# Keys of batches 2 to 4: projected in float16 with tokens on partitions, and turned by the DMA

## The chip, the core and the metric

One core of one Trainium2 chip runs the whole kernel. The metric is device microseconds of that core. The engines are TensorE (PE, with PEld for its weight loads), VectorE (DVE), ScalarE (ACT), GpSimd (POOL) and SyncE (SP), whose queue issues every DMA of this kernel.

## The reference

```python
kv_pool = kv.reshape(B, H // 4, 4, W // 4, 4, C).mean(axis=(2, 4))   # 384x32 -> 96x8 = 768 tokens
k = v = kv_pool.reshape(B, -1, C) @ w_sr                              # 768 x 128 per batch
a = softmax(q @ k.T / sqrt(C))                                        # q: 12288 x 128 per batch
x = (a @ v)                                                           # 4 x 12288 x 128
out = gelu_erf(x @ w_in) @ w_out                                      # 128 -> 2048 -> 128
```

There are 4 batches. The keys (which are the values too) are 768 rows of 128 per batch, made from 12288 pixels by a mean over 4x4 and one 128x128 projection. Everything is float32; the kernel writes its large products as three float16 products of high and low halves.

## The kernel before

A tile is 512 query rows, so a batch has 24 tiles and the kernel 96, numbered `i` = 0 to 95. A tile's work is spread over 16 slots, `f` = 0 to 15, one slot for each 128-wide block of the hidden layer. `slots(i)` yields the work in the order in which each engine gets it. In a slot PE computes one hidden block of tile `i` (`mlp_in`, L765 to L767, three matmuls of 512 columns) and one output block of six slots ago (`mlp_out`, L828 to L830). Scores of tile `i+2` stand in slots 3, 6 and 9, and the first score of tile `i+3` in slot 13 (`score`, L681, six matmuls of 384 columns); the attention product of tile `i+1` stands in slots 10 to 12 (`av`, L741). Every engine works through its own queue in that order, and an instruction that waits holds up what is queued behind it.

A tile's query rows have their own chain: `q_load` (slot 1, L451), the largest value by DVE (`q_max`, slot 5, L479), three passes on POOL that make halves (`q_split`, L502 to L504), a transpose by DMA (`q_turn`, slot 9, L527), and the first score in slot 13 of the same tile `i`. SP also carries the four transposes of the attention weights of a tile (`attn_turn`, L729: two in slot 12, one in slot 15, one in slot 4 of the next tile), the transposes of the output (`o_turn`, L464), the output's stores (L860) and the loads of the next batch's pixels (`kv_load`, L247).

Keys of batch 1 of 4 are made in the kernel's start by a list written out by hand (`START`, tiles 0 to 2). The keys of batches 2 to 4 are made beside the tiles of the batch before, by a table of (tile, slot) that `at` fills (L984 to L1005). With `i0` the second tile of the batch before, for each of six parts `h` of 128 tokens: `kv_load` at tile `i0+2h` slot 1, `kv_sum` on POOL at `i0+2h+1` slot 1, `kv_turn` at `i0+2h+2` slot 2 and `kv_key` at the same tile, slot 11. `kv_turn` (L356) is a float32 transpose on PE, which ACT copies with the factor 1/16 (L358). `kv_key` (L365) is a float32 matmul with `w_sr` as weights, which DVE copies into `kT` (L366), so that channels stand on partitions and tokens along the row. Then `kv_max` (L373) takes the largest value of each channel, and `kv_bound` spreads the largest of all to all partitions: a diagonal matrix on DVE (L380), a float32 matmul by ones (`across`, L386), a reduction on DVE (L391). `kv_high` and `kv_low` (L420, L425) make float16 halves with channels on partitions, as the scores take them, and `kv_val` (L432) is one transpose by DMA of 12 blocks, which makes the halves with tokens on partitions, as `av` takes them.

The PSUM buffer `ps_t` is single, and `kv_turn`, `kv_key` and `across` share it.

Of the kernel before, what the change touches and what calls it, by code (L numbers as in the profile page):

```python
# [16 lines left out]
ALU = mybir.AluOpType  # L17
AX = mybir.AxisListType
# [126 lines left out]
def pooled_attention_mlp(  # L145
# [24 lines left out]
    T = 512  # L170
# [3 lines left out]
    HALVES = (H // P) * 2  # L174
# [20 lines left out]
    kv_h = kv.rearrange("b (h i a) (j w) c -> b h a i j (w c)", i=P // WK, a=R, j=WK)  # L195

    const = ctx.enter_context(tc.tile_pool(name="const", bufs=1))
    stage = ctx.enter_context(tc.tile_pool(name="stage", bufs=6))
# [13 lines left out]
    op = ctx.enter_context(tc.tile_pool(name="op", bufs=1))  # L212
# [28 lines left out]
    st = {}  # L241
# [95 lines left out]
    def kv_sum_part(b, h, i, eng):  # L337
        t = st["kv", b, h][i]
        u = prep.tile([P, 4 * C], F32, tag=f"u{i}", name=f"u_{b}_{h}_{i}")
        eng.tensor_tensor(u, t[:, : 4 * C], t[:, 4 * C :], op=ALU.add)  # L340
        eng.tensor_tensor(u[:, : 2 * C], u[:, : 2 * C], u[:, 2 * C :], op=ALU.add)
        eng.tensor_tensor(u[:, :C], u[:, :C], u[:, C : 2 * C], op=ALU.add)
        st["u", b, h, i] = u[:, :C]
        if i == 1:
            y = prep.tile([P, C], F32, tag=f"y{h % 2}", name=f"y_{b}_{h}")
            eng.tensor_tensor(y, st.pop(("u", b, h, 0)), st.pop(("u", b, h, 1)), op=ALU.add)
            st["y", b, h] = y

    def kv_sum(b, h, eng):

        for i in range(2):
            kv_sum_part(b, h, i, eng)

    def kv_turn(b, h, pool=ps_t, tag="ps_t"):
        ps = pool.tile([P, T], F32, tag=tag, name=f"pp_{b}_{h}")
        nc.tensor.transpose(ps[:, :P], st.pop(("y", b, h)), ident)  # L356
        pT = prep.tile([P, P], F32, tag=f"pT{h % 2}", name=f"pT_{b}_{h}")
        nc.scalar.mul(pT, ps[:, :P], 1.0 / (R * R))  # L358
        st["pT", b, h] = pT

    def kv_key(b, h, pool=ps_t, tag="ps_t", mul=nc.vector.tensor_scalar_mul):
        if h == 0:
            st["kT", b] = prep.tile([P, KEYS], F32, tag="kT", name=f"kT_{b}")
        ps = pool.tile([P, T], F32, tag=tag, name=f"pk_{b}_{h}")
# [619 lines left out]
    def at(i, f, *op):  # L984
        extra.setdefault((i, f), []).append(op)

    for b in range(1, B):
        i0 = TPB * (b - 1) + 1
        for h in range(HALVES):
            i = i0 + 2 * h  # L990
            at(i, 1, "kv_load", b, h)
            at(i + 1, 1, "kv_sum", b, h)
            at(i + 2, 2, "kv_turn", b, h)
            at(i + 2, 11, "kv_last", b, h)
        i1 = i0 + 2 * HALVES + 2
        at(i1, 11, "kv_top", b)
        at(i1, 11, "kv_bound", b, 0)
        at(i1 + 1, 2, "kv_bound", b, 1)
        at(i1 + 1, 11, "kv_bound", b, 2)
        at(i1 + 1, 11, "kv_bound", b, 3)  # L1000
        at(i1 + 1, 12, "mlp_scale", b)
        at(i1 + 1, 12, "out_scale", b)
        at(i1 + 2, 11, "kv_hi", b)
        at(i1 + 2, 12, "kv_lo", b)
        at(i1 + 3, 11, "kv_val", b)  # L1005

    def slots(i):

# [69 lines left out]
    with tc.manual_schedule():  # L1078
        engines = {"dve": nc.vector, "pool": nc.gpsimd}
        copies = {"act": nc.scalar.copy, "dve": nc.vector.tensor_copy}  # L1080
        muls = {"act": nc.scalar.mul, "dve": nc.vector.tensor_scalar_mul,
                "pool": nc.gpsimd.tensor_scalar_mul}
        by = {
            "q_load": q_load, "w_sr": lambda: nc.sync.dma_start(w_sr_sb, w_sr),
            "kv_in": kv_in, "kv_add": lambda h, n=0, m=1, e="dve": kv_add(h, n, m, engines[e]), "kv_pool": kv_pool,
            "kv_pool_out": lambda h, e: kv_pool_out(h, copies[e]),
            "kv_flip": kv_flip, "kv_flip_out": lambda h, e: kv_flip_out(h, copies[e]),
            "kv_nat": kv_nat, "kv_nat_out": lambda n, e: kv_nat_out(n, copies[e]),
            "kv_key": kv_key_first, "kv_key_out": lambda h, e: kv_key_out(h, copies[e]),
            "w_load": w_load, "w_single": w_single, "w_max": w_max, "w_sum": w_sum,  # L1090
            "w_scale": lambda i, step, e="dve": w_scale(i, step, engines[e]),
            "w_hi": lambda j, e: w_hi(j, muls[e]), "w_lo": w_lo,
            "q_turn_first": q_turn_first, "q_out_first": lambda e: q_out_first(copies[e]),
            "score_part": score_part, "evac_part": evac_part, "exp_part": exp_part,
            "turn_part": turn_part,
            "turn_out_part": lambda c, n, e: turn_out_part(c, n, copies[e]),
            "av_part": av_part,
            "parts": lambda step, e="dve": parts(step, engines[e]),
            "join_first": lambda c, e: join_first(c, muls[e]), "join_second": join_second,
            "x_turn": x_turn, "x_first": lambda n, e: x_first(n, copies[e]),  # L1100
            "q_max": q_max, "q_scale": lambda t, e="dve": q_scale(t, engines[e]),
            "q_turn": q_turn, "q_sigma": lambda t, e="dve": q_sigma(t, engines[e]),
            "q_split": q_split, "q_hi": lambda t, e: q_hi(t, muls[e]), "q_lo": q_lo,
            "kv_max": lambda n: kv_max(0, n, 2),
            "kv_high": lambda n, e: kv_high(0, n, 2, muls[e]),
            "kv_bound": lambda b, step, e="dve": (
                kv_bound(b, step) if b else kv_bound(b, step, 2, ps_h, "ps_h", engines[e])),
            "kv_val": kv_val, "mlp_scale": lambda b, e="dve": mlp_scale(b, engines[e]),
            "out_scale": lambda b, e="dve": out_scale(b, engines[e]), "warm": warm,
            "kv_load": kv_load, "kv_sum": lambda b, h: kv_sum(b, h, nc.gpsimd),  # L1110
            "kv_turn": kv_turn, "kv_last": kv_key, "kv_top": kv_max, "kv_hi": kv_high,
            "kv_lo": kv_low, "exp": exp,
            "recips": lambda t, c, n, e="dve": recips(t, c, n, engines[e]),
            "attn_hi": lambda t, c, e="dve": attn_hi(t, c, muls[e]),
            "attn_lo": attn_lo, "attn_turn": attn_turn,
            "x_hi": lambda t, e="dve": x_hi(t, muls[e]), "x_lo": x_lo,
            "score": score, "evac": evac, "mlp_in": mlp_in, "gelu": gelu,
            "gelu_hi": lambda t, p, e="act": gelu_hi(t, p, muls[e]), "rest": rest, "mlp_out": mlp_out, "av": av,
            "o_out": lambda t, e="act": o_out(t, muls[e]), "o_planes": o_planes, "o_turn": o_turn, "o_join": o_join,
            "o_last": o_last,  # L1120
        }
# [37 lines left out]
```

## Time and profile before

| | |
|---|---|
| three timed runs | 2785.69, 2785.78, 2786.09 us |
| median | 2785.78 us |
| span of the profiled execution | 2784.1 us |
| busy: PE, ACT, DVE, POOL | 100%, 90%, 84%, 31% of the span |
| TensorE's granted clock | full speed in all 40 slices |
| DMA engines, mean busy share | 43% of 16 engines |

The profile has the span of its execution, from the first to the last instruction, and no time around it; the median of the timed runs is 1.68 us above that span. "Busy" of PE counts a matmul from its issue to its modelled end, and matmuls overlap, so the cost of a matmul to the queue is the distance between the starts of neighbours and not its duration.

### The profile page before, as it was taken

What the parts mean: (1) busy time and instruction counts of PE and PEld (TensorE: products, weight loads), DVE (VectorE), ACT (ScalarE), POOL (GpSimd) and SP (SyncE); (2) the same over time, 40 slices, a digit from 0 to 9 for tenths busy, and PEclk for the clock granted to TensorE, in tenths of its full rate; (3) what the DMA queues carried; (4) which work ended last, traced back from release to release, by engine and by line L of the source; (5) the groups of instructions that cost most, each with busy time, mean ns of one, the idle gap of its engine ahead of it and who ended that gap; (6) DMA issues with size and microseconds to landing.
All of it is one profiled execution on the core that took longest, in us unless ns stands there. A gap on an engine that the chain in (4) does not pass through costs nothing.

```text
span 2784.1 us, 38177 instructions
## 1 busy us (share of the span) xinstructions
PE 2777.5 (100%) x13720; PEld 1338.0 (48%) x13720; DVE 2349.7 (84%) x3449; ACT 2514.5 (90%) x3419; POOL 867.0 (31%) x826
## 2 busy tenths in 40 slices
PE   9999999999999999999999999999999999999999
PEld 6444444444444444444444444444444444444445
DVE  7888888888888888898888888889888888888786
ACT  7899999999989999998999999899999999899997
POOL 3344442323244343323224343422222232222221
PEclk9999999999999999999999999999999999999999
DMA  7444444344454445344444444433444434343342
GB/s 226 108 105 106 107 108 97 84 106 90 96 117 113 108 104 111 90 91 98 98 106 108 107 106 113 101 95 91 99 95 89 97 89 95 88 99 91 93 89 54
DMA packets 844910, 283.08 MB, mean 102 GB/s; under 512 B 807216, under 2 KB 809776, under 8 KB 843952
## 3 DMA queue, kind: packets, MB, share of 16 engines
q1 hardware_dynamic: 844720, 280.65, 43.2%
q8 instruction: 107, 1.75, 0.3%
q14 instruction: 83, 0.68, 0.1%
HBM read 54.59 MB, written 25.17 MB: 29 GB/s over the span
## 4 chain that ended last, share of the span: by engine, by line
PE 98%; DMA 1%; DVE 0%; POOL 0%; issue 0%; ACT 0%; SPq 0%; POOLq 0%
PE s L681 13%; PE px L741 13%; PE h L765 12%; PE h L766 12%; PE h L767 12%; PE po L830 12%; PE po L829 12%; PE po L828 11%; PE po L819 0%; PE h L762 0%; PE po L806 0%; DMA row<-in_kv_dram 0%; PE s L568 0%; DMA q_v<-q_u 0%; PE warm L325 0%
## 5 line engine op out<-in xcount | busy, mean ns | idle before, releaser
L780 ACT ACTIVATE g<-h,hs 128x512 f32<-128x512 f32 x1520 | 995.2, 681 | 214.6 <-PE h L767 177.1
L788 DVE SCALAR_TENSOR_TENSOR gl<-g,gs,gh 128x1024 f16<-128x1024 f32 x760 | 1003.3, 1333 | 16.1 <-ACT gh L784 8.7
L784 ACT ACTIVATE gh<-g,gs 128x1024 f16<-128x1024 f32 x747 | 857.7, 1148 | 24.2
L766 PE MATMUL h<-xl,wi_h 128*128 128x512 f16 x1520 | 576.1, 379 | 0.0
L767 PE MATMUL h<-xh,wi_l 128*128 128x512 f16 x1520 | 576.1, 379 | 0.0
L765 PE MATMUL h<-xh,wi_h 128*128 128x512 f16 x1520 | 576.1, 379 | 0.0
L829 PE MATMUL po<-gl,wo_h 128*128 128x512 f16 x1504 | 570.0, 379 | 0.0
L830 PE MATMUL po<-gh,wo_l 128*128 128x512 f16 x1504 | 570.0, 379 | 0.0
L828 PE MATMUL po<-gh,wo_h 128*128 128x512 f16 x1504 | 570.0, 379 | 0.0
L502 POOL TENSOR_TENSOR q<-q,qi 128x512 f32<-128x512 f32 x93 | 96.8, 1041 | 1483.1 <-DVE qi L494 1314.1
L692 DVE TENSOR_SCALAR_CACHE_REDUCE sn<-s,sg 128x768 f32<-128x768 f32 x380 | 384.8, 1013 | 75.3 <-PE s L681 74.4
L681 PE MATMUL s<-k,q_v 128*128 128x384 f16 x2280 | 432.7, 326 | 0.1
L720 DVE SCALAR_TENSOR_TENSOR a<-sn,r,a 128x768 f16<-128x768 f32 x380 | 406.1, 1069 | 13.0
L741 PE MATMUL px<-aT,v 128*128 128x512 f16 x1710 | 415.3, 379 | 0.0
L700 ACT ACTIVATE sn<-sn,nm 128x768 f32<-128x768 f32 x380 | 350.9, 924 | 1.2
L681 PEld LDWEIGHTS <-q_v 128*128 128x128 f16 x2280 | 223.0, 98 | 189.0 <-issue 2.9
L741 PEld LDWEIGHTS <-v 128*128 128x128 f16 x1710 | 167.2, 98 | 202.2 <-issue 1.0
L709 DVE TENSOR_SCALAR r<-sum 128x2 f32<-128x2 f32 x183 | 41.4, 226 | 245.8 <-ACT sn L700 245.8
L716 DVE TENSOR_SCALAR a<-sn,r 128x768 f16<-128x768 f32 x370 | 241.6, 653 | 6.9 <-DVE r L712 0.6
L472 POOL COPY o<-o_v 128x512 uint16<-128x512 uint16 x190 | 156.0, 865 | 277.1 <-DMA o_v<-o_u 271.4
L767 PEld LDWEIGHTS <-wi_l 128*128 128x128 f16 x1520 | 148.7, 98 | 179.3
L830 PEld LDWEIGHTS <-wo_l 128*128 128x128 f16 x1504 | 147.2, 98 | 177.5
(171 smaller groups left out, 2254.0 us busy)
## 6 DMA issues: line engine op xcount, KB each, us to landing
q<-in_q_dram SPq DMA_DIRECT2D x96, 256.0 KB, 3.0
out_dram<-o SPq DMA_DIRECT2D x95, 256.0 KB, 2.0
kv<-in_kv_dram SPq DMA_DIRECT2D x72, 256.0 KB, 4.5
aT<-a SPq DMA_TRANSPOSE x380, 3.2
row<-in_kv_dram SPq DMA_DIRECT2D x5, 1024.0 KB, 11.2
w<-in_moe_w_out_dram SPq DMA_DIRECT2D x2, 1024.0 KB, 8.7
q_v<-q_u SPq DMA_TRANSPOSE x95, 2.8
o_v<-o_u SPq DMA_TRANSPOSE x95, 2.7
```

What stands on the lines that cost most here:

```text
L681: nc.tensor.matmul(ps[:, n, :KH], lhs[:, c], rhs[:, n * KH : (n + 1) * KH], start=rhs is kh and lhs is qh, stop=lhs is ql,)
L720: nc.vector.scalar_tensor_tensor(a[:, 1, :], st.pop(("s", t, c)), st["r", t][:, c : c + 1], a[:, 0, :], op0=ALU.mult, op1=ALU.subtract,)
L741: nc.tensor.matmul(ps, v[:, w, :], aT[:, :, o + k, :], start=k == 0 and i == 0, stop=k == KB - 1 and i == 2,)
L765: nc.tensor.matmul(ps, wi_h[:, fs], xh, start=True, stop=False)
L766: nc.tensor.matmul(ps, wi_h[:, fs], xl, start=False, stop=False)
L767: nc.tensor.matmul(ps, wi_l[:, fs], xh, start=False, stop=True)
L780: nc.scalar.activation(g, ps, AF.Gelu, scale=st["hs", t // TPB] if t > 0 else 1.0)
L784: mul(st["gh", t, p], st["g", t, p], st["gs", t // TPB])
L788: nc.vector.scalar_tensor_tensor(gl, st["g", t, p], st["gs", t // TPB], st["gh", t, p], op0=ALU.mult, op1=ALU.subtract)
L828: nc.tensor.matmul(ps, wo_h[:, f, :], gh[:, e, :], start=f == 0, stop=False)
L829: nc.tensor.matmul(ps, wo_h[:, f, :], gl[:, e, :], start=False, stop=False)
L830: nc.tensor.matmul(ps, wo_l[:, f, :], gh[:, e, :], start=False, stop=f == FB - 1)
```

## The change

All of it concerns the keys of batches 2 to 4. The six parts of pooled sums go into one tile `y` (6 blocks of 128 tokens). After the last sum, `kv_size` (DVE) takes the largest value for each token and block and makes a power of two from it; `kv_split` (POOL, three passes over 768 columns) scales the sums by it and makes float16 halves; `kv_turn` is now one DMA transpose of 12 blocks; `kv_project` is 18 float16 matmuls of 128 columns, in two groups of 12 and 6, whose weights are the turned halves and whose moving operand is a half of `w_sr`, so that tokens stand on partitions, and DVE copies each group with its scale. The largest key of all is spread by `every`: a DMA stores 128 values to DRAM, and a second one reads them back to every partition. `kv_halves` makes the halves with tokens on partitions, and `kv_back`, a DMA transpose of 12 blocks, makes those with channels on partitions. `sr_max` and `sr_split`, once, in tiles 3 and 4, split `w_sr` in the same way, with one `every`. The places in the table: `kv_size` and `kv_split` in tile `i1 = i0+12`, `kv_turn` in `i1+1`, `kv_project` and `kv_top` in `i1+2`, `kv_bound` in `i1+3`, `kv_halves` in `i1+4`, `kv_back` in `i1+5`. Loads and sums keep their tiles, and the last step keeps its tile too (`i0+17`).

```diff
+    def power(x, tag, name, eng=nc.vector):
+        n = x.shape[1]
+        e = small.tile([P, n], I32, tag=tag + "e", name=name + "_e")
+        i = small.tile([P, n], I32, tag=tag + "i", name=name + "_i")
+        eng.tensor_scalar_max(x, x, 2.0**-90)
+        nc.vector.tensor_scalar(e, x.bitcast(I32), 0x7F800000, None, op0=ALU.bitwise_and)
+        eng.tensor_scalar(i, e, -1.0, float(268 << 23), op0=ALU.mult, op1=ALU.add)
+        return e.bitcast(F32), i.bitcast(F32)
+    def kv_size(b):
+        m = small.tile([P, KB], F32, tag="ym", name=f"ym_{b}")
+        nc.vector.tensor_reduce(
+            m, st["y", b], axis=AX.X, op=ALU.max, apply_absolute_value=True
+        )
+        e, st["yi", b] = power(m, "y", f"y_{b}")
+        st["yc", b] = small.tile([P, KB], F32, tag="yc", name=f"yc_{b}")
+        nc.vector.tensor_scalar_mul(st["yc", b], e, st["srs"])
+    def kv_split(b):
+        y = st.pop(("y", b))
+        t = stage.tile([P, 4, KB, C], F16, tag="stage", name=f"yu_{b}")
+        i = st.pop(("yi", b)).unsqueeze(2).to_broadcast([P, KB, C])
+        nc.gpsimd.tensor_tensor(y, y, i, op=ALU.mult)
+        nc.gpsimd.tensor_copy(t[:, 0], y)
+        nc.gpsimd.tensor_tensor(t[:, 1], y, t[:, 0], op=ALU.subtract)
+        st["yu", b] = t
-    def kv_turn(b, h, pool=ps_t, tag="ps_t"):
-        ps = pool.tile([P, T], F32, tag=tag, name=f"pp_{b}_{h}")
-        nc.tensor.transpose(ps[:, :P], st.pop(("y", b, h)), ident)
...
+    def kv_turn(b):
+        t = st["yu", b]
+        nc.sync.dma_start_transpose(
+            t[:, 2:].rearrange("p e k c -> p (e k) c"),
+            t[:, :2].rearrange("p e k c -> p (e k c)"),
+        )
-    def kv_key(b, h, pool=ps_t, tag="ps_t", mul=nc.vector.tensor_scalar_mul):
...
-        nc.tensor.matmul(ps[:, :P], w_sr_sb, st.pop(("pT", b, h)), start=True, stop=True)
-        mul(st["kT", b][:, h * P : (h + 1) * P], ps[:, :P], 1.0)
+    def kv_project(b, k0, k1):
...
+        yT, w = st["yu", b][:, 2:], st["srh"]
+        for k in range(k0, k1):
+            for i, (e, m) in enumerate(((0, 0), (0, 1), (1, 0))):
+                nc.tensor.matmul(
+                    ps[:, k - k0], yT[:, e, k], w[:, m], start=i == 0, stop=i == 2
+                )
+        c = st["yc", b][:, k0:k1].unsqueeze(2).to_broadcast([P, k1 - k0, C])
+        nc.vector.tensor_tensor(st["kn", b][:, k0:k1], ps[:, : k1 - k0], c, op=ALU.mult)
+    def every(x, name):
+        d = dram.tile([P, 1], F32, tag="d", name=name + "_d")
+        r = small.tile([P, P], F32, tag="diag", name=name + "_r")
+        nc.sync.dma_start(d, x)
+        nc.sync.dma_start(r, d.rearrange("p o -> o p").to_broadcast([P, P]))
+        return r
+    def kv_top(b):
+        st["mx", b] = small.tile([P, 2], F32, tag="mx", name=f"mx_{b}")
+        nc.vector.tensor_reduce(
+            st["mx", b][:, :1], st["kn", b].rearrange("p k c -> p (k c)"), axis=AX.X,
+            op=ALU.max, apply_absolute_value=True,
+        )
+        st["dg", b] = every(st["mx", b][:, :1], f"km_{b}")
+    def kv_back(b):
+        st["k", b] = keys.tile([P, 2, KEYS], F16, tag="k", name=f"k_{b}")
+        nc.sync.dma_start_transpose(
+            st["k", b].rearrange("p n (k c) -> p (n k) c", c=P),
+            st["v", b].rearrange("p k c -> p (k c)"),
+        )
...
-            at(i + 2, 2, "kv_turn", b, h)
-            at(i + 2, 11, "kv_last", b, h)
...
+        i1 = i0 + 2 * HALVES
+        at(i1, 2, "kv_size", b)
+        at(i1, 11, "kv_split", b)
+        at(i1 + 1, 2, "kv_turn", b)
+        at(i1 + 2, 2, "kv_project", b, 0, 4)
+        at(i1 + 2, 11, "kv_project", b, 4, KB)
+        at(i1 + 2, 11, "kv_top", b)
+        at(i1 + 3, 11, "kv_bound", b, 2)
+        at(i1 + 3, 11, "kv_bound", b, 3)
+        at(i1 + 3, 12, "mlp_scale", b)
+        at(i1 + 3, 12, "out_scale", b)
+        at(i1 + 4, 11, "kv_halves", b, 0)
+        at(i1 + 4, 12, "kv_halves", b, 1)
+        at(i1 + 5, 11, "kv_back", b)
+    at(3, 2, "sr_max")
+    at(4, 2, "sr_split")
```

## Rows read from the trace of the kernel before

**Rows 1.** The page's head and part 1: busy us (share of span) xinstructions

```profile
span 2784.1 us, 38177 instructions
PE 2777.5 (100%) x13720; PEld 1338.0 (48%) x13720; DVE 2349.7 (84%) x3449; ACT 2514.5 (90%) x3419; POOL 867.0 (31%) x826
```

**Rows 2.** The chain that ended last, by engine

```profile
PE 98%; DMA 1%; DVE 0%; POOL 0%; issue 0%; ACT 0%; SPq 0%; POOLq 0%
```

**Rows 3.** Waits of PE: line, releaser: us in total, times, longest

```profile
PE pp L282 <- DMA row<-in_kv_dram: 1.6, 2, 1.4
```

**Rows 4.** PE in order of time, tile 35: start us, us

```profile
1049.84 0.27 PE L356 MATMUL pp<-ident,y 128*128 128x128 f32 x1
1049.95 0.38 PE L828 MATMUL po<-gh,wo_h 128*128 128x512 f16 x1
...
1067.12 0.38 PE L365 MATMUL pk<-pT,w_sr_sb 128*128 128x128 f32 x2
1067.34 0.38 PE L828 MATMUL po<-gh,wo_h 128*128 128x512 f16 x1
```

**Rows 5.** Groups by line and shape, PE and PEld: busy us, mean ns

```profile
L365 PE MATMUL pk<-pT,w_sr_sb 128*128 128x128 f32 x36 | 6.9, 274 | 0.0
L356 PE MATMUL pp<-ident,y 128*128 128x128 f32 x18 | 4.9, 273 | 0.0
L806 PEld LDWEIGHTS <-gh 128*128 128x128 f16 x128 | 10.2, 98 | 1.1
```

**Rows 6.** PE in order of time, last tile, first and twelfth of L806

```profile
2764.76 0.22 PE L806 MATMUL po<-wo_h,gh 128*128 128x128 f16 x1
...
2765.37 0.22 PE L806 MATMUL po<-wo_l,gh 128*128 128x128 f16 x1
```

**Rows 7.** SP in order of time, tiles 34 to 36: start us, us

```profile
1042.41 8.73 SPq L729 DMA_TRANSPOSE aT<-a  x3
1051.19 0.58 SPq L451 DMA_DIRECT2D q<-in_q_dram  x1
...
1064.69 1.30 SPq L527 DMA_TRANSPOSE q_v<-q_u  x1
...
1070.78 10.46 SPq L729 DMA_TRANSPOSE aT<-a  x3
1081.29 0.58 SPq L451 DMA_DIRECT2D q<-in_q_dram  x1
1085.94 1.40 SPq L729 DMA_TRANSPOSE aT<-a  x1
...
1095.37 1.31 SPq L527 DMA_TRANSPOSE q_v<-q_u  x1
```

**Rows 8.** PE in order of time, tile 36, slots 12 and 13

```profile
1099.51 0.38 PE L767 MATMUL h<-xh,wi_l 128*128 128x512 f16 x1
1100.01 1.15 PE L681 MATMUL s<-k,q_v 128*128 128x384 f16 x6
```

**Rows 9.** DVE in order of time, tiles 35 and 36

```profile
1067.95 1.35 DVE L716 TENSOR_SCALAR a<-sn,r 128x768 f16<-128x768 f32 x1
...
1085.83 0.68 DVE L479 TENSOR_REDUCE qm<-q 128x4 f32<-128x512 f32 x1
```

**Rows 10.** Groups by line and shape, DVE: busy, mean ns | idle before

```profile
L716 DVE TENSOR_SCALAR a<-sn,r 128x768 f16<-128x768 f32 x370 | 241.6, 653 | 6.9 <-DVE r L712 0.6
L709 DVE TENSOR_SCALAR r<-sum 128x2 f32<-128x2 f32 x183 | 41.4, 226 | 245.8 <-ACT sn L700 245.8
```

**Rows 11.** Groups by line and shape, POOL, the longest pass of `q_split`

```profile
L504 POOL TENSOR_TENSOR q_u<-q,q_u 128x512 f16<-128x512 f32 x93 | 184.9, 1988 | 7.4
```

**Rows 12.** DMA issues: xcount, KB each, median us from issue to landing

```profile
out_dram<-o SPq DMA_DIRECT2D x2, 64.0 KB, 1.6
w_sr_sb<-in_w_sr_dram SPq DMA_DIRECT2D x1, 64.0 KB, 9.4
v<-k SPq DMA_TRANSPOSE x4, 3.8
```

More of the change, by code (lines that the diff above doesn't have):

```diff
@@ L197, in pooled_attention_mlp @@
     const = ctx.enter_context(tc.tile_pool(name="const", bufs=1))
+    dram = ctx.enter_context(tc.tile_pool(name="dram", bufs=2, space=bass.MemoryType.DRAM))
     stage = ctx.enter_context(tc.tile_pool(name="stage", bufs=6))
@@ L344, in kv_sum_part @@
         if i == 1:
-            y = prep.tile([P, C], F32, tag=f"y{h % 2}", name=f"y_{b}_{h}")
-            eng.tensor_tensor(y, st.pop(("u", b, h, 0)), st.pop(("u", b, h, 1)), op=ALU.add)
-            st["y", b, h] = y
+            if h == 0:
+                st["y", b] = prep.tile([P, KB, C], F32, tag="y", name=f"y_{b}")
+            eng.tensor_tensor(
+                st["y", b][:, h], st.pop(("u", b, h, 0)), st.pop(("u", b, h, 1)), op=ALU.add
+            )
     def kv_sum(b, h, eng):
@@ new lines, in kv_turn @@
+    def kv_turn(b):
[5 more added lines that the diff above has]
+    def kv_project(b, k0, k1):
+        if k0 == 0:
+            st["kn", b] = prep.tile([P, KB, C], F32, tag="kT", name=f"kn_{b}")
+        ps = ps_t.tile([P, T], F32, tag="ps_t", name=f"pk_{b}_{k0}").rearrange(
+            "p (k c) -> p k c", c=C
+        )
[7 more added lines that the diff above has]
+        nc.vector.tensor_tensor(st["kn", b][:, k0:k1], ps[:, : k1 - k0], c, op=ALU.mult)
@@ new lines, in every, with sr_max, sr_split @@
+    def every(x, name):
[4 more added lines that the diff above has]
+        return r
+    def sr_max():
+        m = small.tile([P, 1], F32, tag="srm", name="srm")
+        nc.vector.tensor_reduce(m, w_sr_sb, axis=AX.X, op=ALU.max, apply_absolute_value=True)
+        st["srm"] = every(m, "srm")
+    def sr_split():
+        m = largest(st.pop("srm"), "srm")
+        e, i = power(m, "sr", "sr")
+        st["srs"] = const.tile([P, 1], F32, name="srs")
+        nc.vector.tensor_scalar_mul(st["srs"], e, 2.0**-28 / (R * R))
+        st["srh"] = const.tile([P, 2, C], F16, name="srh")
+        nc.vector.tensor_scalar_mul(st["srh"][:, 0], w_sr_sb, i)
+        nc.vector.scalar_tensor_tensor(
+            st["srh"][:, 1], w_sr_sb, i, st["srh"][:, 0], op0=ALU.mult, op1=ALU.subtract
+        )
@@ new lines, in kv_top, with kv_halves @@
+    def kv_top(b):
[3 more added lines that the diff above has]
+            op=ALU.max, apply_absolute_value=True,
+        )
+        st["dg", b] = every(st["mx", b][:, :1], f"km_{b}")
+    def kv_halves(b, n):
+        if n == 0:
+            st["v", b] = keys.tile([P, 2 * KB, C], F16, tag="v", name=f"v_{b}")
+            nc.vector.tensor_scalar_mul(st["v", b][:, :KB], st["kn", b], st["kinv", b])
+        else:
+            nc.vector.scalar_tensor_tensor(
+                st["v", b][:, KB:], st["kn", b], st["kinv", b], st["v", b][:, :KB],
+                op0=ALU.mult, op1=ALU.subtract,
+            )
@@ L368, in kv_max @@
+    def kv_back(b):
[3 more added lines that the diff above has]
+            st["v", b].rearrange("p k c -> p (k c)"),
+        )
     def kv_max(b, n=0, parts=1):
@@ L989, in pooled_attention_mlp @@
         for h in range(HALVES):
-            i = i0 + 2 * h
-            at(i, 1, "kv_load", b, h)
-            at(i + 1, 1, "kv_sum", b, h)
-            at(i + 2, 2, "kv_turn", b, h)
-            at(i + 2, 11, "kv_last", b, h)
[L995 to L1005, printed above, removed]
+            at(i0 + 2 * h, 1, "kv_load", b, h)
+            at(i0 + 2 * h + 1, 1, "kv_sum", b, h)
+        i1 = i0 + 2 * HALVES
[14 more added lines that the diff above has]
+    at(4, 2, "sr_split")
     def slots(i):
@@ L1110, in pooled_attention_mlp @@
             "kv_load": kv_load, "kv_sum": lambda b, h: kv_sum(b, h, nc.gpsimd),
-            "kv_turn": kv_turn, "kv_last": kv_key, "kv_top": kv_max, "kv_hi": kv_high,
-            "kv_lo": kv_low, "exp": exp,
+            "kv_turn": kv_turn, "kv_top": kv_top, "kv_size": kv_size, "kv_split": kv_split,
+            "kv_project": kv_project, "kv_halves": kv_halves, "kv_back": kv_back,
+            "sr_max": sr_max, "sr_split": sr_split, "kv_lo": kv_low, "exp": exp,
             "recips": lambda t, c, n, e="dve": recips(t, c, n, engines[e]),
```

6 lines of the change are left out of this document (removed).

## The prediction

> **What bounds the kernel now.** I read the busy shares first: PE is busy for 2777.5 of 2784.1 us, ACT for 90%, DVE for 84% [rows 1]. A busy PE is not proof of a bound, so the chain of waits came next: 98% of it is PE [rows 2]. The waits of PE say the same from the other side: its largest entry is 1.6 us for the first pixels at the start [rows 3], and nothing comparable follows. So PE's queue sets the time: a matmul that leaves it is worth the distance between the starts of its neighbours, one that enters costs the same, and work of DVE, ACT, POOL or SP costs nothing until it makes PE wait. The last thing to read is therefore where PE nearly waits. In tile 36 a matmul starts at 1099.51 and the first score of the next query rows at 1100.01, 0.50 us later where 0.22 is the usual distance [rows 8, 4]: a gap of 0.28 us in a query chain that had only just been in time. That gap is the place to watch.
>
> **What PE loses.** A batch has six transposes `kv_turn`, six products `kv_key` and one `across`. In tile 35 the transpose starts at 1049.84 and its successor at 1049.95: 0.11 us. The product starts at 1067.12, in two passes, and its successor at 1067.34: 0.22 us [rows 4]. That the mean of one is 273 or 274 ns [rows 5] is pipeline depth, not cost to the queue. 18 rows of the transpose and 36 passes of the product [rows 5] are three batches of six. `across` has the same form as `kv_key`, so three more at 0.22. Sum: 18 x 0.11 + 18 x 0.22 + 3 x 0.22 = 1.98 + 3.96 + 0.66 = 6.6 us.
>
> **What PE gains.** 18 float16 matmuls of 128 columns per batch, 54 in all, each with weights of its own. The nearest rows are the matmuls of the last tile, same shape and type, weights changed each time: from the first to the twelfth, 2764.76 to 2765.37, eleven steps in 0.61 us, so 0.055 us each [rows 6]. 54 x 0.055 = 3.0 us. From below, a quarter of a 512-column matmul's 0.22 is the same 0.055 [rows 4]. From above, one float32 pass of 128 columns is 0.11 [rows 4], which would make 5.9 us and a net of 0.7. I take 0.055, the row of the same form.
>
> The Trainium skill says otherwise here ("TensorE: Matmul & The Clock Gate", section "Back-to-back issue gap"): in a sustained stream of weight load and matmul, 128 columns take about 81 ns each, since the weights' load counts too. The last tile's row contradicts it at 55 ns; by the page the 54 would take 4.4 us and the net would be 2.2 us.
>
> Net on PE: 6.6 - 3.0 = 3.6 us off, if nothing else reaches PE.
>
> **What the others get, and what hides it.** ACT loses 18 copies, DVE 18 copies of 128 columns, and it gets two larger ones per batch: no engine that bounds, so zero.
>
> `kv_size` adds on DVE a reduction over 768 columns: `q_max` takes 0.68 for 512 [rows 9], so 1.0 as an estimate, and four short operations of some 0.23 each, as the row on 2 columns has it [rows 10], together 1.9 us at slot 2 of tile `i1`. Behind it wait the attention's halves and `q_max` of that tile. DVE's own idle time covers it: it waits 245.8 us for ACT's exponentials in 183 places, two to a tile [rows 10], so some 2.6 a tile. Without that cover the query chain of the tile is 1.9 late; its transpose is issued at 1064.69 in the undisturbed tile 35 and at 1095.37 in the late tile 36 [rows 7], 30.7 us later, where the first transposes of the attention in two tiles are 28.4 apart [rows 7]; so an undisturbed tile has about 2 us in hand over the late one. It fits, barely.
>
> `kv_split` is three passes over 768 columns on POOL. The longest pass of `q_split` takes 1.99 us for 512 [rows 11]; three at 1.5 times that are at most 9 us. POOL is busy 31% [rows 1]. But it slows DVE: with POOL's sums beside it `attn_hi` took 1.35 us in tile 35 [rows 9] where 0.65 is the mean [rows 10]. That is why SP needed 10.46 us for three transposes of the attention there against 8.73 a tile earlier, and why the next `q_load` went out at 1081.29, 30.1 us after the one before [rows 7]. So tile `i1`, which has no sums of its own, becomes like tile 35, and tile `i1+1` like tile 36. There are 18 stretches with such sums before, and the waits of PE list none of them [rows 3]. I allow 0.1 us per batch, 0.3 in all; the ends are 0 and, if each of the three is as late again as tile 36 was early, about 2 us each.
>
> The Trainium skill has a rule on this ("SBUF — State Buffer", section "SBUF: two separate sides"): DVE and GpSimd take a shared port pair by an exclusive lock, and the loser blocks for the whole instruction. By it a DVE operation beside a 3 us pass could lose up to 3 us, not 0.7. The trace shows 1.35 for 0.65 and so half as much again at most; the sum stays with the row.
>
> `kv_turn` as a DMA is a second transpose of 12 blocks per batch, like `v<-k`, 3.8 us to landing [rows 12], issued at slot 2 of `i1+1`. SP there is free from 1081.87 to 1085.94, between `q_load` and the next transpose [rows 7], and an issue takes 1.4 [rows 7]. PE reads the result a tile later. Zero. `kv_back` stands where `kv_val` stood. Zero.
>
> `every` is the one new wait: SP issues the store when DVE has the maximum, in slot 11 of `i1+2`, and holds the second DMA, and all behind it, until the store has landed: the output's store, the transposes of slots 12 and 15, then `q_load`. How much room is there? Undisturbed, the stretch from the first of the three transposes to `q_load` is 8.73 us, of which three issues of 1.40 are 4.2 [rows 7]; 4.5 are waiting. The copy and the reduction ahead of the store take about 1.5 us of DVE (0.68 x 1.5 and a half more), and the two issues and the output's store some 1.2. That leaves 1.8 us for the landing before `q_load` moves. The late tile 36 had its `q_load` 1.7 us later in its three transposes (10.46 - 8.73) and lost only 0.28. And its data, issued at 1081.29, were used by DVE at 1085.83, after 4.5 us [rows 7, 9]. So a landing up to about 1.8 + 1.7 = 3.5 us is covered. A store's landing in the trace: 1.6 us for 64 KB; the longest of 64 KB, a load in the crowd of the start, 9.4 [rows 12]. Here 512 bytes go in tile `i1+2`, where no pixels are loaded, so I take 1.6 to 2, hidden. In tile 3 `sr_max` does the same once, just behind four loads of pixels; by tile 36, SP has 4 us free at that slot, and I count up to 1 us of risk and no mean.
>
> **Sum.** -6.6 + 3.0 + 0.3 = -3.3 us. Against the profiled execution: 2784.1 - 3.3 = 2780.8 of span. The median is 1.68 us above that span, which nothing here changes: 2785.78 - 3.3 = 2782.5 us, 0.12% less.
>
> **Rivals.**
>
> *Partly given back.* The query chain behind `kv_split`, or behind SP's new wait, ends 0.3 to 1 us late in two tiles per batch: 3 x 2 x 0.6 = 3.6 us, so no gain, 2785.8 or a little under. For it: the gap in tile 36, a chain with nothing in hand. Against it: 18 stretches with POOL's sums left no entry among PE's waits [rows 3].
>
> *Weights bound the projection.* If each of the 54 matmuls waits for its own weights, it costs the load's 98 ns [rows 5]: 5.3 us instead of 3.0, so 2784.8. Against it: the same loads of 98 ns stand under steps of 55 ns in the last tile.
>
> *SP's round trip, the case that ends slower.* The store's landing is as long as the 9.4 us row. SP is then held 9.4 - 3.5 = 5.9 us too long in `i1+2`; `q_load` is late by that, the query chain too, and PE stands still: 3 x 5.9 = 17.7 us, less 3.6: 2799.9. It decides from a landing above 3.5 + 1.2 = 4.7 us, where the three stalls use up the 3.6. For it: 128 values of 4 bytes, one from each partition, have no row in the trace. Against it: the transfer is tiny, and 128 times as many bytes land in 1.6.
>
> *More than predicted.* By both rows the matmuls cost 0.055 us at the least, so the net is at most 3.6, and with the gap of 0.28 gone 3.9: 2781.9. No way to a gain of 0.2% that I can find.
>
> **How the numbers follow.** A difference of 0.2%, 5.6 us, is about what a measurement can tell from none. The forecast, 2781.8 to 2783.5, has 0.64; partly given back 0.17; weights 0.05; SP's round trip 0.08, 0.01 of it still within 0.2% (a landing under 6.6); a cause that I have not seen 0.06, either way. The first three are all within 0.2%. So faster 0.03, same 0.87, slower 0.10. The range takes in the forecast, the weights and the given-back case, and leaves out the round trip: 2781.7 to 2786.2.
>
> **What would show it.** Right: in the profile after, the distances of tiles with `kv_key` and `kv_turn` shrink by 0.22 and 0.11, 18 matmuls of 128 columns stand at 0.055 us from start to start, PE's waits stay as short as before, and SP's second DMA of `every` goes out some 2 us after the first. Wrong: a gap ahead of the first score in tiles `i1+1` or `i1+3` of more than 0.5 us, or steps of 0.1 us in the projection, or a store that lands after more than 4 us.

## The result and the profile after

The changed kernel takes 2803.19 us (median of 5 runs, 2799.85 to 2804.73), the kernel before 2786.05 beside it (2785.69 to 2786.27): ratio 1.0058 [1.0046, 1.0071]. Forecast were 2782.5 and a range up to 2786.2. It is 17.1 us slower, and the time lies near the rival that ends slower, SP's round trip (2799.9).

The page of the kernel after: head, part 1, the DMA queue of part 3 (packets, MB, share), and the chain by engine.

```profile
span 2801.5 us, 38159 instructions
PE 2780.2 (99%) x13714; PEld 1334.2 (48%) x13714; DVE 2373.3 (85%) x3457; ACT 2512.7 (90%) x3401; POOL 886.3 (32%) x835
...
q1 hardware_dynamic: 850576, 282.10, 49.4%
...
PE 92%; DVE 3%; DMA 2%; ACT 1%; POOL 1%; issue 0%; SPq 0%; POOLq 0%; DVEq 0%
```

PE is still busy for 99%, but the chain is down from 98% [rows 2] to 92% of PE: the rest runs through other engines and through transfers. Queue q1 is busy for 49.4% instead of 43.2% with hardly more bytes (280.65 MB before), which matters below. Where PE waits (line, releaser: us in total, times, longest), against the entry of [rows 3] (the last two lines belong to the kernel's start):

```profile
PE s L781 <- DVE sn L792: 8.4, 3, 4.0
PE px L841 <- DMA aT<-a: 3.3, 2, 3.0
PE s L668 <- DVE kT L336: 2.0, 1, 2.0
PE pp L283 <- DMA row<-in_kv_dram: 1.9, 1, 1.9
```

Three long waits of the score matmul, one in each of batches 2 to 4, and one of 3.0 us in tile 3, where the largest weight is spread. SP's own waits say for what: L420 is the load of `every`, L419 its store.

```profile
SPq L420 <- DMA km_d<-mx: 23.0, 3, 9.1
SPq L419 <- DVE mx L443: 14.8, 3, 5.3
SPq L420 <- DMA srm_d<-srm: 7.6, 1, 7.6
```

The DMA issues (xcount, KB each, median us to landing), which answer to [rows 12]:

```profile
aT<-a SPq DMA_TRANSPOSE x380, 3.7
q_v<-q_u SPq DMA_TRANSPOSE x95, 3.1
o_v<-o_u SPq DMA_TRANSPOSE x95, 3.2
...
km_d<-mx SPq DMA_DIRECT2D x3, 0.5 KB, 7.6
...
srm_d<-srm SPq DMA_DIRECT2D x1, 0.5 KB, 8.5
```

The store of 512 bytes lands after 7.1 to 9.5 us in the three batches; I had taken 1.6 to 2. SP in order of time in batch 2 (start us, us), against [rows 7]:

```profile
505.07 0.33 SPq L419 DMA_DIRECT2D km_d<-mx  x1
512.69 0.32 SPq L420 DMA_DIRECT2D km_r<-km_d  x1
513.10 0.38 SPq L960 DMA_DIRECT2D out_dram<-o  x1
513.59 6.84 SPq L829 DMA_TRANSPOSE aT<-a  x3
520.48 0.85 SPq L551 DMA_DIRECT2D q<-in_q_dram  x1
```

and DVE's first use of those query rows, idle 4.43 us before it:

```profile
523.92 0.69 DVE L579 TENSOR_REDUCE qm<-q 128x4 f32<-128x512 f32 x1 [4.43 <-DMA q<-in_q_dram]
```

From 505.07 to 512.69 SP issues nothing; the query load goes out 15.4 us after the store. In batch 4 it is worst. PE in order of time there, then a window of 5 us (length; busy us and count of PE, PEld, DVE, ACT and POOL; granted clock; DMA share; GB/s):

```profile
1901.15 0.38 PE L867 MATMUL h<-xh,wi_l 128*128 128x512 f16 x1
1905.48 2.08 PE L781 MATMUL s<-k,q_v 128*128 128x384 f16 x6 [3.96 <-DVE sn L792]
1907.36 0.63 PE L928 MATMUL po<-gh,wo_h 128*128 128x512 f16 x1
1907.78 0.63 PE L929 MATMUL po<-gl,wo_h 128*128 128x512 f16 x1
```

```profile
1905.00:1910.00 5.00, 4.51 (x13) 1.86 (x13) 5.00 (x8) 0.00 (x0) 4.86 (x5) 0.50 0.00 0
```

The gap is 1905.48 - 1901.15 - 0.22 = 4.11 us, and after it the granted clock is 0.50, the lower of the two levels (1.2 of 2.4 GHz): matmuls start 0.42 apart instead of 0.22. The six scores, the six matmuls behind them and the next six take some 2.5 us more than at full clock. So one late transfer is paid for twice.

**The account.** Comparing tile by tile when PE starts the first product with the values (`px`), after against before (a jump is put down to the tile in whose slots PE works then): the start +3.6; tiles 4 to 14 and their like in later batches -0.11 or -0.22 each, as the transposes and products leave; +0.67 for twelve new float16 matmuls in tiles 15, 39 and 63; and jumps at tile 3 of +3.1, at 16 and 17 of +3.1, at 40 and 41 of +2.7, at 64 and 65 of +6.8 (0.1 of each of these three is PE's own: `across` is gone, six matmuls came; the stalls are 3.0, 2.6 and 6.7). With PE's own -3.6 as forecast, that leaves some 2 us in gaps of less than 0.5. The 3.6 at the start lie ahead of every instruction of the change: the first pixels are used at 9.21 us instead of 8.59, and from 10 to 12 us the granted clock is 0.50. The two of the five runs at 2800 would fit a start without this; the experiments' profiles show -0.1 to +0.8 there, with the clock at 1.00.

### The profile page after: what moved, and what is told of

Its sections match the earlier page's. It is cut to its first block, busy times and chain, and to the rows that moved or that the text cites. A ratio compares the mean times of both kernels' runs of the same rounds, so it can differ in the third digit from the quotient of the medians.

```text
span 2801.5 us, 38159 instructions
## 1 busy us (share of the span) xinstructions
PE 2780.2 (99%) x13714; PEld 1334.2 (48%) x13714; DVE 2373.3 (85%) x3457; ACT 2512.7 (90%) x3401; POOL 886.3 (32%) x835
## 3 DMA queue, kind: packets, MB, share of 16 engines
q1 hardware_dynamic: 850576, 282.10, 49.4%
## 4 chain that ended last, share of the span: by engine, by line
PE 92%; DVE 3%; DMA 2%; ACT 1%; POOL 1%; issue 0%; SPq 0%; POOLq 0%; DVEq 0%
PE s L781 13%; PE px L841 12%; PE h L867 11%; PE h L866 11%; PE h L865 11%; PE po L929 11%; PE po L930 11%; PE po L928 11%; DVE gl L888 1%; DVE a L820 1%; DMA aT<-a 1%; PE po L919 0%; PE h L862 0%; ACT sn L800 0%; DVE a L816 0%
## 5 line engine op out<-in xcount | busy, mean ns | idle before, releaser
L888 DVE SCALAR_TENSOR_TENSOR gl<-g,gs,gh 128x1024 f16<-128x1024 f32 x760 | 1004.6, 1335 | 15.4 <-ACT gh L884 8.6
L809 DVE TENSOR_SCALAR r<-sum 128x2 f32<-128x2 f32 x183 | 57.4, 314 | 236.3 <-ACT sn L800 236.3
```

The source lines that it names most:

```text
L888: nc.vector.scalar_tensor_tensor(gl, st["g", t, p], st["gs", t // TPB], st["gh", t, p], op0=ALU.mult, op1=ALU.subtract)
```

## The experiments

The theory: `every` costs by its store's landing, because SP stands still until then. The rival: something else of the new float16 path does it (VectorE's and GpSimd's new work, the projection, the second transpose).

**e1, the largest key spread by TensorE again.** Of the spreads only the weight's in tile 3 still goes by a store and a load.

```
-        st["dg", b] = every(st["mx", b][:, :1], f"km_{b}")
+        st["dg", b] = diagonal(st["mx", b][:, :1], f"km_{b}")
...
+        at(i1 + 3, 2, "kv_bound", b, 1)
```

> The changed kernel, but the largest key of a batch is spread as before (diagonal matrix, float32 matmul by ones); the spread of w_sr's maximum in tile 3 stays with the two DMAs. Theory (SP is held for the 7 to 9.5 us that the 512-byte store takes to land, the next query rows are loaded late, PE stands still two tiles on): in the changed kernel's tile-by-tile ledger the stalls behind the three stores are about 3.0, 2.7 and 6.8 us, 12.5 in all; they go, three float32 matmuls (0.66 us) come back, and the stall of some 3 us in tile 3 stays. From 2803.2 that gives 2791 us, or 2788 if the loss of 3.6 us at the start is absent. Rival (the key chain's other new work, kv_size, kv_split or the new transpose, makes the query chain late): the stalls in tiles i1+2 and i1+3 stay and the time is 2803 or a little more.

Measured: 2790.55 (2789.95 to 2792.40), ratio 1.0017 [1.0008, 1.0026]. The jumps at tiles 16, 40 and 64 are gone (+0.33 each, the six matmuls); tile 3 keeps its jump (+3.8), and tile 4 has one of +1.5 that the change's profile does not show. The median falls by 12.6 us; by the tiles, 11.6 of it are the three spreads.

**e2, the spread by a transfer alone.** The kernel before, float32 path and all, with only `across` replaced.

```
-            st["dg", b] = diagonal(mx[:, :1], f"km_{b}")
+            st["dg", b] = (every if b else diagonal)(mx[:, :1], f"km_{b}")
```

> The kernel before with one part of the change alone: the largest key of batches 2 to 4 goes by a store and a load, in the same tile and slot as in the changed kernel; transposes and projection stay float32 on PE. Theory (SP held by the store's landing): stalls of 2.5 to 7 us behind each of the three stores, less 0.66 us for the matmuls by ones: 2786.0 + 9 to 13 - 0.7 = 2794 to 2798 us. Rival (the float16 part is to blame): within 1 us of 2786.

Measured: 2797.16 (2793.68 to 2801.94), 1.0042 [1.0028, 1.0056]. PE's waits, and two DMA issues:

```profile
PE s L691 <- DVE sn L702: 7.9, 3, 3.8
```

```profile
aT<-a SPq DMA_TRANSPOSE x380, 3.2
...
km_d<-mx SPq DMA_DIRECT2D x3, 0.5 KB, 7.7
```

The same three waits without any float16 path, jumps of +3.9, +1.8 and +5.5 (behind the first gap, of 2.3 us, the granted clock is at 0.50 from 522 to 524 us here, where it stays at 1.00 in the change): the rival falls as the main cause. The attention's transposes land in 3.2 us here, as before, and in 3.7 with the float16 path: a second difference, set aside at this point.

**e3, SP no longer waits.** The changed kernel with store and load apart: the store in slot 13, the load in slot 5 of the next tile, the weight's in tiles 3, 4 and 5.

```
+        at(i1 + 2, 13, "kv_out", b)
+        at(i1 + 3, 5, "kv_in_all", b)
...
+    at(4, 2, "sr_in")
+    at(5, 2, "sr_split")
```

> The changed kernel with store and load of the spread apart: the store is issued in slot 13 of tile i1+2, the load in slot 5 of the next tile, so that SP never waits for a landing; for w_sr the store in tile 3 and the load in tile 4. Theory (only the hold of SP cost time): no stall of PE above 0.5 us behind the stores, and the net on PE of the prediction, 6.6 - 3.0 = 3.6 us, shows: 2786.0 - 3.6 = 2782.4 us, up to 2786 if the start loses its 3.6 us again. Rival (the transfers themselves, or the float16 path, disturb the query chain): above 2790.

Measured: 2789.06 (2787.77 to 2792.64), 1.0013 [1.0004, 1.0022]: 14 us better than the change and yet missed by 3. SP in batch 2, the landings of the last two of these, and the wait of PE that is left:

```profile
503.19 0.86 SPq L416 DMA_DIRECT2D km_d<-mx  x1
507.01 1.43 SPq L838 DMA_TRANSPOSE aT<-a  x1
508.49 0.88 SPq L560 DMA_DIRECT2D q<-in_q_dram  x1
```

```profile
q<-in_q_dram SPq DMA_DIRECT2D x1, 256.0 KB, 7.2
aT<-a SPq DMA_TRANSPOSE x1, 7.6
```

```profile
PE s L790 <- DVE sn L801: 2.8, 3, 1.4
```

SP is free, and the query load goes out 5.3 us after the store instead of 15.4. But the store, which lands in 10.5 us here, ends at 513.7, and the query rows land at 515.7, after it, and DVE first uses them at 515.70. Their load took 7.2 us here, 7.3 and 7.9 in the other two batches, where 3.2 is this kernel's median. So the slow store delays what is queued behind it too, not only SP. (The second part of the miss is e6's.)

**e4, the store by itself.** Beside the kernel before, in batch 4 where it disturbs nothing, stores of five shapes, three of each: 4 bytes from each of 128 partitions into 512 adjoining bytes, the same 64 and 512 bytes apart, and 64 and 512 bytes from each.

```
+        w = (1, 1, 1, 16, 128)[k]
+        wide = (1, 16, 128, 16, 128)[k]
+        d = dram.tile([P, wide], F32, tag=f"d{k}", name=f"dd{k}_{n}")
+        nc.sync.dma_start(d[:, :w], x[:, :w])
```

> The kernel before with a small store from a constant to an unused place in DRAM in slot 11 of 15 tiles of batch 4, five shapes three times each; nothing waits for them. Shapes: 4 bytes per partition to 512 adjoining bytes (as in the change); 4 bytes to rows 64 bytes apart; 4 bytes to rows 512 bytes apart; 64 bytes per partition, adjoining; 512 bytes per partition, adjoining. Theory (128 writes into the same 512 bytes are taken one after the other): the first lands in 7 to 9 us, the second in less, the third, fourth and fifth in about 2. Rival A (a write of 4 bytes is slow wherever it goes): the first three alike at 7 to 9, the fourth and fifth at about 2. Rival B (the place in the tile, or what is in the queue, makes it slow): all five alike.

Measured, in one run (2786.14). The DMA issues of five windows that hold one store each, in the order of the shapes:

```profile
dd<-px SPq DMA_DIRECT2D x1, 0.5 KB, 9.2
...
dd<-px SPq DMA_DIRECT2D x1, 0.5 KB, 1.4
...
dd<-px SPq DMA_DIRECT2D x1, 0.5 KB, 1.4
...
dd<-px SPq DMA_DIRECT2D x1, 8.0 KB, 1.4
...
dd<-px SPq DMA_DIRECT2D x1, 64.0 KB, 1.5
```

The adjoining ones landed after 9.2, 10.0 and 7.9 us, the other twelve after 1.4 to 1.5, 64 KB among them. The size is not it, nor the 4 bytes: it is 128 separate 4-byte writes next to one another.

**e5, do the values or the place matter?** I first read e4 by the row that groups its nine 4-byte stores, a median of 1.4 us over three shapes, and took the adjoining store to be fast there. e5 was built on that misreading: values of the weight against a constant, early and late tiles, with and without a load behind it. A median over a group with mixed shapes hides a third of it.

```
+        nc.vector.tensor_scalar_mul(x[:, :w], (w_sr_sb if k else ones)[:, :w], 1.0)
```

> The kernel before with small stores again, nothing waiting for them. The probe with a constant source landed in 1.4 us in all five shapes, so neither 4 bytes nor adjoining bytes alone explain the 7 to 10 us. Now: the constant and 128 different values (a column of w_sr), 4 bytes per partition to 512 adjoining bytes, in tiles 19 to 22; the constant and the different values in batch 4; the different values to rows 64 and 512 bytes apart; 64 and 512 bytes per partition; and the different values in tiles 30, 40 and 50 with a later load of them, as in the change. Theory (a value that changes what stands in memory is what is slow, piece by piece): the constant lands in 1.4 everywhere, the different values in 7 to 10 where the bytes adjoin, in less where they lie apart or fill 512 bytes. Rival A (the stretch of the program): all stores of tiles 19 to 50 are slow, all of batch 4 fast. Rival B (the later load of the same bytes): only the stores of tiles 30, 40 and 50 are slow.

Measured, in one run (2786.32): the thirteen adjoining stores landed after 7.5 to 10.5 us, whatever the values, the tile or the load behind; 1.4 to 1.5 for the twelve others. Values and place are out. The time stayed where it was, though each of the thirteen had transfers queued behind it: the output's store and two of the attention's transposes, which landed after 8.3 to 11.9 us where this kernel's medians are 2.1 and 3.2. Behind the store of tile 40:

```profile
out_dram<-o SPq DMA_DIRECT2D x1, 256.0 KB, 10.1
aT<-a SPq DMA_TRANSPOSE x2, 9.9
```

SP did not wait for the store, and the query load went out 11.5 us after that store, when it had landed, and took 3.2 us. So those transfers had the room; a slow store harms where SP waits for it, as in the change, or where a transfer without that room stands behind it, as the query load does in e3.

**e6, both spreads by TensorE.** e1, with the weight's spread by `diagonal` and `across` as well, so that no slow store is left.

```
-        st["srm"] = every(m, "srm")
+        st["srm"] = diagonal(m, "srm")
...
+    at(3, 11, "sr_across")
```

> The changed kernel without any store to DRAM: both spreads, the batches' and w_sr's, by a diagonal matrix and a float32 matmul by ones on PE; all else of the change stays. Theory (the landing of the stores is the whole loss): against the run with the batches' spread on PE the stalls of tiles 3 and 4 (3.8 and 1.5 us in its ledger) go and one float32 matmul of 0.22 us comes: 2790.6 - 5.3 + 0.2 = 2785.5 us; by the prediction's terms alone (6.6 - 0.66 - 0.22 of PE work gone, 3.0 come) 2785.8 - 2.7 = 2783.1. Rival (the rest of the change has a price of its own): above 2787.

Measured: 2786.68 (2785.82 to 2787.32), 1.0001 [0.9992, 1.0010]. All jumps are gone, and the median is 16.5 us under the change's, but PE's own gain of 2.7 us (3.6 less 4 x 0.22 for the spreads) isn't there: it goes in gaps of 0.2 to 0.7 us, and PE's waits name transposes (`q_v` 0.8 us, `aT` 0.3). In every kernel so far with the float16 path the transposes of the attention, the queries and the output land later than before, those of tiles far from the change too; those of the keys do not (3.8 us both times). One thing all these kernels share: their new tiles, of 32 and 512 bytes in a partition ahead of the staging rows and a few small ones, move every SBUF tile behind them. The query, attention and output tiles began 256 bytes past a multiple of 512 and now begin at 448.

**e7, the placement of before, and e8, the placement alone.** e7 is e6 with two unused tiles that bring the offsets back; e8 is the kernel before with two that bring the changed kernel's offsets.

```
+        pad = const.tile([P, 120], F32, name="pad")
+        pad = small.tile([P, 88], F32, tag="pad", name="pad2", bufs=1)
```

> The kernel of e6 (float16 path, both spreads by TensorE) with two unused pads, of 480 and of 352 bytes in a partition, so that the tiles behind them begin at the same offset from a multiple of 512 bytes as in the kernel before: staging rows at 448 instead of 480, keys at 128 instead of 160, query, attention and output tiles at 256 instead of 448. Theory (where in SBUF the tiles lie is what makes every transposing transfer land later in the kernels with the float16 path): the attention's transposes land in 3.2 us again (3.7 in e6), those of the queries' halves in 2.8 (3.1), those of the output's in 2.7 (3.2); the small gaps of TensorE go and the time is 2782.8 to 2784.5, since 2786.05 less the 2.7 us of TensorE's instructions saved is 2783.3. Rival (the float16 path's own traffic delays the others, or the gaps come from VectorE's and GpSimd's new work): the landings stay at 3.7, 3.1 and 3.2 and the time at 2786 to 2787.5.

> The kernel before, with nothing of the change but its placement: two unused pads, of 544 and of 160 bytes in a partition, so that the tiles lie at the same offsets as in the changed kernel (480, 160 and 448 bytes past a multiple of 512 instead of 448, 128 and 256). Theory (placement): the attention's transposes land in 3.7 us instead of 3.2, the queries' in 3.1 instead of 2.8, the output's in 3.2 instead of 2.7, and the time rises by 1 to 4 us, to 2787 to 2790, since e6 lost about 3 us beside what its instructions cost. Rival (placement does nothing): the landings of the kernel before, and 2785.6 to 2786.5.

The landings in e7, then in e8:

```profile
aT<-a SPq DMA_TRANSPOSE x380, 3.2
q_v<-q_u SPq DMA_TRANSPOSE x95, 2.8
o_v<-o_u SPq DMA_TRANSPOSE x95, 2.7
```

```profile
aT<-a SPq DMA_TRANSPOSE x380, 3.7
q_v<-q_u SPq DMA_TRANSPOSE x95, 3.2
o_v<-o_u SPq DMA_TRANSPOSE x95, 3.2
```

Both ways as the theory has it. e7 takes 2783.98 (2783.24 to 2785.16, 11 runs), 2.7 less than e6; e8 takes 2787.41 (2786.57 to 2789.78, 11 runs), 1.5 more than the 2785.95 of the kernel before. The ratios, 0.9993 [0.9984, 1.0002] and 1.0005 [0.9996, 1.0015], settle neither alone; but no run of e7 is above the lowest of the 27 before (2785.29). In e7 most of PE's gain of 2.7 us is there, some 2: it lies below both kernels, 0.07% under the one before. Its profile has one new stall of 1.0 us, at the first score in slot 13 of tile 37, whose query transpose landed just before it, after 5.2 us instead of 2.8; e6 has one of 0.6 in the same place, and the kernel before has none there.

**e9, a wait of SP with a quick store.** The kernel before, and in the place where e2 has its spread, a store of 64 bytes per partition and a load that waits for it, whose values nothing uses.

```
+        nc.vector.tensor_copy(c[:, :16], x.to_broadcast([P, 16]))
+        nc.sync.dma_start(d, c[:, :16])
+        nc.sync.dma_start(r, d.rearrange("(o p) c -> o (p c)", p=8)[:1].to_broadcast([P, P]))
```

> The kernel before, with its largest key spread by TensorE as before, and beside that, for batches 2 to 4 and in the place where e2 has its spread by a transfer, a store and a load on SP whose values nothing uses: VectorE copies each partition's maximum to 16 places, the store writes 64 bytes of each partition instead of 4, and the load (64 KB) waits for it. So SP waits as in e2, only the store's shape differs. Theory (the shape of the store is what costs: 128 writes of 4 bytes into the same 512 land in 7 to 10 us, 64 bytes each in 1.4): the store lands in 1.4 to 2.5 us, SP is free 3.5 us after the store at the latest, TensorE shows no gap of over 1 us at tiles 16, 40 and 64, and the time is 2785.5 to 2787.5. Rival (any load that waits on SP for a store's landing costs TensorE, whatever the shape): gaps of 2.5 us and more in the three batches as in e2, and 2792 to 2798.

Measured: 2785.56 (2785.20 to 2786.13, 11 runs), 0.9999 [0.9990, 1.0008]. SP in batch 2:

```profile
499.18 0.34 SPq L400 DMA_DIRECT2D km_w<-km_c  x1
500.61 0.33 SPq L401 DMA_DIRECT2D km_r<-km_w  x1
501.02 0.38 SPq L871 DMA_DIRECT2D out_dram<-o  x1
501.51 7.41 SPq L740 DMA_TRANSPOSE aT<-a  x3
508.97 0.57 SPq L462 DMA_DIRECT2D q<-in_q_dram  x1
```

A store, a wait and a load in the place of e2's, 1.43 us apart instead of 7.7, and PE's schedule has no jump at tiles 16, 40 and 64. A wait of SP is free here; a landing of 7 us is not.

**e10, the change itself in the placement of before.** The pads of e7 in the changed kernel.

> The changed kernel whole, its spreads by transfers as they are, with the two unused pads of e7 (tiles at 448, 128 and 256 bytes past a multiple of 512 again). Theory (two causes that add: the slow 4-byte stores in tiles 3, 16, 40 and 64, and the placement of all tiles behind the new ones): the transposes land in 3.2, 2.8 and 2.7 us, the stores as late as before (7 to 10 us), and the time falls by what e7 fell against e6, 2.7 us, to 2798 to 2801.5, with the jumps of TensorE's schedule at tiles 3, 16, 40 and 64 still there. Rival (the jumps are so large only because the other transfers were slowed by placement): it falls further, below 2797. Second rival (the stores' stalls leave slack that hides the placement's cost): it stays at 2802 to 2804.

Measured: 2795.82 (2793.92 to 2798.41), 1.0035 [1.0022, 1.0049]: 7.4 less than the change, where I expected 2.7. The time is in the first rival's range, but the jumps stay. Transposes land in 3.2 and 2.8 us, the stores in 6.9 to 8.9, and PE waits

```profile
PE s L785 <- DVE sn L796: 7.2, 3, 3.7
PE px L845 <- DMA aT<-a: 3.3, 1, 3.3
```

By the tiles, 3.2 of the 7.4 are the start (+0.4 here, +3.6 in the profile of the change), 2.5 are jumps (tile 3 +3.4, 16 and 17 +2.2, 40 +1.9, 64 and 65 +5.6), 1.7 the small gaps. So the three later stalls are shorter here; that placement is what lengthens them in the change is not shown: these are single profiles, and e2, in the same placement as e10, has +3.9 in batch 2. That the start belongs to placement is not shown: the kernels with the same offsets, e1, e3, e6 and e8, have +0.2 to +0.8 there.

**e11 and e12, which offsets.** The kernel before with a pad of 256 or of 64 bytes ahead of the query, attention and output tiles: offsets 0 and 320.

```
+    nc.gpsimd.memset(small.tile([P, 64], F32, tag="pad", name="pad", bufs=1)[:, :1], 0.0)
```

> The kernel before with one unused pad of 256 bytes in a partition ahead of the query, attention and output tiles, which then begin at a multiple of 512 bytes instead of 256 past it; rows and keys stay where they were. Theory (the transposes write and read pieces of 256 bytes in a partition, 128 values of 2 bytes, and are slower where a piece crosses a boundary of 256 bytes): landings of 3.2, 2.8 and 2.7 us as before, and 2785.5 to 2786.7. Rival (256 past a multiple of 512 is special, or any move costs): 3.4 us or more for the attention's, and 2786.5 to 2789.

> The kernel before with one unused pad of 64 bytes instead: query, attention and output tiles begin at 320 bytes past a multiple of 512. Theory (pieces of 256 bytes that cross a boundary of 256 are slower): 3.5 to 3.8 us for the attention's transposes, 3.0 to 3.3 for the queries' and the output's, 2786.5 to 2789. Rival (only the offset of 448 is slow, or the boundary is 64 bytes): 3.2, 2.8 and 2.7 us, 2785.5 to 2786.5.

The attention's landings in e11, then in e12:

```profile
aT<-a SPq DMA_TRANSPOSE x380, 3.2
```

```profile
aT<-a SPq DMA_TRANSPOSE x380, 3.7
```

and 2785.67 against 2787.82 us in one run each. 0 and 256 are quick, 320 and 448 slow: multiples of 256 bytes, as expected (128 past one was not tried). The Trainium skill has this in "DMA: Bandwidth & Descriptors", section "How a descriptor splits into AXI transactions": a descriptor is cut into transactions of 256 bytes that must start on a 256-byte boundary, so one that doesn't start there begins with a transaction from the boundary below it. The landings agree (3.2 against 3.7 us); that this is the mechanism inside no run here shows.

## Why the prediction was wrong

**PE loses and PE gains: right.** The tiles' distances shrink by 0.11 and 0.22, and `across` goes. The 54 matmuls were forecast at 0.055 us; twelve of them cost a tile 0.67, so 0.056 each, with weights of their own:

```profile
L408 PE MATMUL pk<-srh,yu 128*128 128x128 f16 x54 | 4.0, 219 | 0.0
```

so the rival with weights at 98 ns falls. The trace agrees with [rows 6] and not with the 81 ns of the Trainium skill ("TensorE: Matmul & The Clock Gate", section "Back-to-back issue gap"). e7 is the check on the sum: the forecast of 2782.5, plus four spreads left on PE at about 0.22, is 2783.4; measured 2783.98.

**`kv_size`, `kv_split`, `kv_turn`, `kv_back`: nothing on PE, as forecast.** In the change's profile tiles 13 to 15 and 18, where they run, show nothing beyond the matmuls, so the price put on `kv_split`, 0.1 us per batch, wasn't needed there. One reading behind it was wrong: 1.35 us for 0.65 is twice, not "half as much again at most", and in each of the three batches one operation of the attention's halves took 1.88 us beside `kv_split`'s last pass. PE did not wait for it. The stall of e7 in tile 37 is in the tile of `kv_split`, but there the query transpose was issued in time (28.8 us after the one before) and landed late; the profile names DVE's `xh`, which ended in the same moment, so a share of `kv_split` is not ruled out. Batches 2 and 4 show none.

**`every`: the step that failed.** It said: "A store's landing in the trace: 1.6 us for 64 KB; the longest of 64 KB, a load in the crowd of the start, 9.4. Here 512 bytes go in tile `i1+2`, where no pixels are loaded, so I take 1.6 to 2, hidden." Measured: 7.1 to 9.5 us in the three batches. The reasoning went by bytes, and the nearest row by bytes had one large piece per partition; the store had 128 pieces of 4 bytes side by side, a shape with no row. The prediction names this as the rival's point ("have no row in the trace") and then lets "128 times as many bytes land in 1.6" outweigh it, at a chance of 0.08. e4 shows the size to be worthless as a guide: 64 KB in 1.5 us, 512 bytes in 7.9 to 10.0.

The room, 3.5 us, was put too small. The landing less PE's idle time at the score behind it is 7.6 - 2.4 = 5.2, 7.1 - 2.1 = 5.0 and 9.5 - 4.0 = 5.5 us in the change, and 5.2 to 5.4 in e10 (5.4, 5.9 and 3.8 in e2). A landing of the forecast 1.6 to 2 us would have been covered either way; it was the landing that failed. By the rival's formula with the landing that was measured, 3 x (7.6 - 3.5) = 12.3 us; the three stalls add up to 3.0 + 2.6 + 6.7 = 12.3. That closeness is luck: the idle time is 8.4 us only, and what the formula doesn't know, the clock at 0.50 behind the 4.11 us gap (some 2.5 us) and the smaller gaps, makes up for the room. With the transposes quick again (e10) the jumps are 2.2, 1.9 and 5.6, less than its 12.3.

**Tile 3: missed.** "Up to 1 us of risk and no mean" for `sr_max`: the same store lands after 8.5 us, and PE's schedule loses 3.1 (3.4 in e10), here by waiting for a transpose of the attention that SP issued late. One transfer's price was wrong in four places.

**A cause not seen: the placement.** Nothing in the prediction asks where the tiles go. New tiles moved the transposes' tiles off a 256-byte boundary: 1.5 us alone (e8), 2.7 with the float16 path (e6 against e7), and up to 7.4 with the stores, the start's 3.2 of it not shown to be placement.

The times of the four combinations, medians in us (the kernel before took 2785.76 to 2786.07 beside them):

| | offsets as changed | offsets as before |
|---|---|---|
| both spreads by transfers | 2803.19 (the change) | 2795.82 (e10) |
| both by TensorE | 2786.68 (e6) | 2783.98 (e7) |

Still open: the start of the change's profile, which the other kernels do not show, and why batch 4's stall is over twice that of batches 2 and 3. Some 2.5 of its 6.7 us are the lower clock, which the change's profile has in no other stall, and its store landed latest (9.5 us); but in e2 the three landed alike (7.6 to 7.7) and batch 4 still lost the most.

## What to carry to other kernels

A tiny store is priced by its pieces, not by its bytes: give each partition at least 64 bytes, or 64 bytes of distance, where anything waits for it or is queued behind it, and where the shape has no row in the trace, weigh the longest landing as seriously as the shortest. When a change adds an SBUF tile, see that the tiles behind it which the DMA transposes still begin at multiples of 256 bytes, and compare the landings of transfers that the change doesn't touch. Bring a suspect operation to the chip by itself, and read it by its own row, never by a median over several shapes.

## What the runs showed of the hardware

- 128 writes of 4 bytes into 512 adjoining bytes of DRAM: 7.5 to 10.5 us to landing in 16 probes, with a constant or varied source, in busy and in quiet tiles. 4 bytes every 64 or 512 bytes: 1.4. 64 bytes per partition: 1.4; 512: 1.5. The Trainium skill says in "DMA: Bandwidth & Descriptors", section "Specifications", that below 512 bytes a transfer is read, modified and written. The slow store agrees, but 4 bytes at a distance of 64 are below 512 as well and land in 1.4, so here the rule alone doesn't tell the slow from the quick.
- While such a store is under way, what is queued behind it lands late: query loads after 7.2 to 7.9 us instead of 3.2 (e3), attention's transposes and output stores after 8.3 to 11.9 instead of 3.2 and 2.1 (48 transfers behind the 16 probes of e4 and e5).
- DMA transposes of tiles at 0 and 256 bytes past a multiple of 512: 3.2 us (attention) and 2.8 (queries); at 320 and 448: 3.7 and 3.1 to 3.2. The queue's share of the span goes from 43.2% to 49.9% by the two pads of e8 alone.
